# Exchanging the two operands of the output projection: weights stand, 512 gated values move

## The chip, the cores and the metric

The kernel runs on one core of a Trainium2 chip. The metric is the device time of one execution in microseconds (us). TensorE (PE) multiplies, its weight loads are listed apart (PEld), VectorE (DVE), ScalarE (ACT) and GpSimd (POOL) do the rest, and SyncE (SP) issues most of the transfers.

## The reference

Three layers follow each other. Only the third, a gated layer, is touched:

```python
def _moe2_ref(x, w_gate, w_val, w_out):
    g = x @ w_gate                       # 256 -> 1536
    silu = g * (1.0 / (1.0 + np.exp(-g)))
    val = x @ w_val
    return (silu * val @ w_out)          # 1536 -> 256

# x: 8 * 3072 tokens of 256 values. Ahead of it stand a spectral filter
# (rfft, times a filter, irfft) and a soft mixture of 8 experts with 4 slots
# each: x = softmax(logits, axis=1) @ slot_out, slot_out of 32 rows.
```

## The kernel before

Phase 1 (about the first 400 us) does the filter and the mixture's logits. On the side it rounds the three weight matrices of the gated layer (`conv`, lines 559 to 597): 36 chunks, 12 of them of `w_out` (index `i == 2`), go through ACT, DVE and POOL and are stored again in DRAM (`wd`, line 595), from where `first` (line 919) fetches `w_out` for phase 2. A short transition computes the slots' outputs times `w_gate` and `w_val`.

Phase 2 is a loop over 576 items `(b, q, G, f)`: 8 batches, 3 times 2 blocks of 512 tokens, and for each block 12 slices `f` of 128 hidden values. 12 items are a group, and a group makes 512 rows of the output. For an item,

- `gv` multiplies the slice of the gate and of the value matrix with the block's weights (two matmuls of 512 columns, lines 986 and 987), and ACT applies the silu (line 989);
- `gate` (DVE, line 995) multiplies both to `h`, and `split` one item later makes of it a rounded part `hi` (ACT, line 1002) and the rest `lo` (DVE, line 1003);
- `proj`, three or four items later (`lag`), multiplies with `w_out`. `wo[f]` holds two parts of it, index 0 the rounded one and index 1 the rest, made by `load_out` (lines 975 and 976) during the first 12 items.

`proj` computes `hi` times both parts of the weights and `lo` times the rounded part. `hi` and `lo` are the stationary operands, 128 tokens at a time (`t` from 0 to 3), and the weights move: 512 columns (both parts side by side) for `hi`, 256 for `lo`. Four PSUM banks `o0` to `o3` collect one group. At the end of a group ACT copies half of a bank (line 1027), DVE adds the other half to it (line 1028), and SP stores the 512 rows in four transfers (line 1031), each of 32 runs of 4 KB.

All engines take their instructions in the order in which the program is written (`manual_schedule`), so `proj(i - 4)` stands between `gv(i)` and `gate(i)`, and what it gives DVE at a group's end stands ahead of `gate(i)` there. The V tile in PSUM has two buffers (line 970): the matmul of line 987 for item `i + 2` waits until `gate(i)` has read the first.

Of the kernel before, what the change touches and what calls it, by code (L numbers as in the profile page):

```python
# [7 lines left out]
F32 = mybir.dt.float32  # L8
# [3 lines left out]
AF = mybir.ActivationFunctionType  # L12
ALU = mybir.AluOpType
# [4 lines left out]
NB, SEQ, D, E = 8, 3072, 256, 32  # L18
NEXP, SPE, FE, FF = 8, 4, 1024, 1536
NJ, NP, NR = 24, 96, 32  # L20
NF = FF // 128
# [58 lines left out]
def spectral_softmoe_glu_kernel(  # L80
# [17 lines left out]
    nc = tc.nc  # L98
    pe, dve, act, pool = nc.tensor, nc.vector, nc.scalar, nc.gpsimd
# [37 lines left out]
    def phase1():  # L137
        with ExitStack() as c1:
# [418 lines left out]
            def flat(a):  # L557
                return a.rearrange("(p a) f -> p (a f)", p=128)

            def conv():  # L560


                cw = 256
                chunks = [(i, c) for i in range(3) for c in range(FF * D // 128 // cw)]
                raws = {}

                def load(n):
                    if n >= len(chunks):
                        return
                    i, c = chunks[n]  # L570
                    raws[n] = cvp.tile([128, cw, 2], I32, tag="raw", name="raw", bufs=2)
                    nc.sync.dma_start(
                        out=raws[n].rearrange("p n k -> p (n k)"),
                        in_=flat((w_gate, w_val, w_out)[i])[:, c * cw:(c + 1) * cw].bitcast(I32),
                    )

                load(0)
                load(1)
                yield
                for n, (i, c) in enumerate(chunks):  # L580
                    raw = raws.pop(n)
                    hf, lw = raw[:, :, 1].bitcast(F32), raw[:, :, 0].bitcast(U32)
                    mag = cvp.tile([128, cw], I32, tag="mag", name="mag", bufs=2)
                    low = cvp.tile([128, cw], I32, tag="low", name="low", bufs=2)
                    act.activation(mag.bitcast(F32), hf, AF.Copy, scale=2.0 ** -112)
                    yield
                    act.activation(low, lw, AF.Copy, scale=2.0 ** -29)
                    act.activation(hf, hf, AF.Sign)
                    yield
                    dve.tensor_scalar(mag, mag, 3, None, ALU.logical_shift_left)  # L590
                    yield
                    pool.tensor_tensor(out=low, in0=mag, in1=low, op=ALU.add)
                    mf = low.bitcast(F32)
                    pool.tensor_tensor(out=mf, in0=mf, in1=hf, op=ALU.mult)
                    nc.sync.dma_start(out=flat(wd[i])[:, c * cw:(c + 1) * cw], in_=mf)
                    load(n + 2)
                    yield
# [55 lines left out]
            for k in range(2):  # L653
# [4 lines left out]
                out=nyq, in_=bass.AP(filt_r.tensor, SEQ // 2 * D, [[1, 128], [128, 2]])  # L658
# [7 lines left out]
            pool.tensor_scalar_mul(nyq, nyq, 0.5)  # L666
            dve.memset(expo, 0.0)
            side, firsts = conv(), first_weights()
            todo = []
            gens, ready = [], []  # L670
# [296 lines left out]
    def phase2(later):  # L967
        cp, g4, v4, wo, c4, build = (later[k] for k in ("cp", "g4", "v4", "wo", "c4", "build"))
        kp = p2.enter_context(tc.tile_pool(name="kp", bufs=3))
        ps_g = p2.enter_context(tc.tile_pool(name="ps_g", bufs=2, space=PSUM))  # L970
        ps_o = p2.enter_context(tc.tile_pool(name="ps_o", bufs=1, space=PSUM))

        def load_out(f):
            st = wo[f][:, 1, :].bitcast(F32)
            act.copy(wo[f][:, 0, :], st)
            pool.tensor_tensor(out=wo[f][:, 1, :], in0=st, in1=wo[f][:, 0, :], op=ALU.subtract)  # L976

        items = [(b, q, G, f) for b in range(NB) for q in range(3) for G in range(2) for f in range(NF)]
        hb, hhi, hlo, acc, sb2 = {}, {}, {}, {}, {}

        def gv(i):
            b, q, G, f = items[i]
            c, fs = f // 4, slice(f % 4 * 128, f % 4 * 128 + 128)
            pg = ps_g.tile([128, 512], F32, tag="G", name="G")
            pv = ps_g.tile([128, 512], F32, tag="V", name="V")
            pe.matmul(out=pg, lhsT=g4[c][:, fs], rhs=c4[b][:, q, G, :])  # L986
            pe.matmul(out=pv, lhsT=v4[c][:, fs], rhs=c4[b][:, q, G, :])  # L987
            s = kp.tile([128, 512], F32, tag="s", name="s")
            act.activation(s, pg, AF.Silu)  # L989
            sb2[i] = (s, pv)  # L990

        def gate(i):
            s, pv = sb2.pop(i)
            h = kp.tile([128, 512], F32, tag="h", name="h")
            dve.tensor_tensor(out=h, in0=pv, in1=s, op=ALU.mult)  # L995
            hb[i] = h

        def split(i):
            h = hb.pop(i)
            hi = kp.tile([128, 512], F32R, tag="hi", name="hi", bufs=LAG + 1)  # L1000
            lo = kp.tile([128, 512], F32R, tag="lo", name="lo", bufs=LAG + 1)
            act.copy(hi, h)  # L1002
            dve.tensor_tensor(out=lo, in0=h, in1=hi, op=ALU.subtract)  # L1003
            hhi[i], hlo[i] = hi, lo

        def proj(i):
            b, q, G, f = items[i]
            hi, lo = hhi.pop(i), hlo.pop(i)
            if f == 0:
                acc[0] = [ps_o.tile([128, 512], F32, tag=f"o{t}", name=f"o{t}") for t in range(4)]  # L1010
            for t in range(4):
                a = acc[0][t]
                ts = slice(128 * t, 128 * t + 128)
                pe.matmul(  # L1014
                    out=a, lhsT=hi[:, ts], rhs=wo[f].rearrange("p k d -> p (k d)"),
                    start=(f == 0), stop=(f == NF - 1), skip_group_check=True,
                )
                pe.matmul(  # L1018
                    out=a[:, D:2 * D], lhsT=lo[:, ts], rhs=wo[f][:, 0, :],
                    start=False, stop=(f == NF - 1), skip_group_check=True,  # L1020
                )
            if f == NF - 1:
                ot = kp.tile([128, 4, D], F32, tag="ot", name="ot", bufs=2)
                for t in range(4):
                    a = acc[0][t]
                    tmp = kp.tile([128, D], F32, tag="tmp", name="tmp", bufs=4)
                    act.copy(tmp, a[:, D:2 * D])  # L1027
                    dve.tensor_tensor(out=ot[:, t, :], in0=a[:, 0:D], in1=tmp, op=ALU.add)  # L1028
                row = b * SEQ + 1024 * q + 16 * G
                for ii in range(4):  # L1030
                    nc.sync.dma_start(
                        out=bass.AP(out.tensor, (row + 4 * ii) * D, [[32 * D, 32], [1, 4 * D]]),
                        in_=ot[32 * ii:32 * ii + 32].rearrange("p t d -> p (t d)"),
                    )

        def lag(i):

            r = i % (6 * NF) - EXP_AT
            if r in (1, 2, 3, 4, 5, 6):
                return (4, 3, 3, 3, 4, 4)[r - 1] if i < len(items) - 6 * NF else LAG  # L1040
            return min(LAG, 3 + i // 10)

        todo = list(range(len(items)))
        gen = build(1)
        for i in range(len(items) + LAG):
            if i < len(items):
                b, q, G, f = items[i]
                if q == 0 and G == 0 and f == 0 and b:
                    for _ in gen:
                        pass  # L1050
                    gen = build(b + 1) if b + 1 < NB else iter(())
                gv(i)
            while todo and todo[0] <= i - lag(i):
                proj(todo.pop(0))
            if i < len(items):
                gate(i)
            if i < NF:
                load_out(i)
            if 0 <= i - 1 < len(items):
                split(i - 1)  # L1060
            if i % 4 == 1 and i > NF:
                next(gen, None)

    with tc.manual_schedule():
        phase1()
        phase2(transition())
        p2.close()
# [32 lines left out]
```

## Time and profile before

| | |
|---|---|
| median of 3 runs | 1491.43 us (1491.24 to 1492.1) |
| the profiled execution, its own time | 1492.65 us |
| its span from the first to the last instruction | 1490.9 us |
| TensorE busy | 1439.6 us (97%) |
| VectorE busy | 1151.7 us (77%) |
| ScalarE busy | 962.5 us (65%) |
| stores of the output | 192 of 128 KB each |

The span is what the profile's views divide; the execution's own time is 1.75 us longer than the span, and lies 1.2 us above the median. A busy engine is not an engine at its peak: matmuls overlap in the records, so the time that one of them takes is read from the distance between starts, not from its own duration.

### The profile page before, as it was taken

Reading aid. Unit: us, or ns where it says so; the run is one execution under the profiler, and the core shown is the slowest. Engines: PE = TensorE matmul, PEld = TensorE weight load, DVE = VectorE, ACT = ScalarE, POOL = GpSimd, SP = SyncE. Lnnn points to the kernel's source line nnn. Section 1 sums busy time; section 2 is a strip of 40 time slices with the busy share of each in tenths; the row PEclk is TensorE's granted clock in tenths of the full one; section 3 lists DMA queues with packets and bytes.
Section 4 is the critical chain, followed back from the end, with each engine's and each line's share of the span. In section 5 each row is a group of like instructions: output and inputs, shape, how many; then the busy total and the mean of one; then the engine's idle time right before and its main releaser. Section 6 shows DMA issues by size and latency. Waiting matters only on the chain.

```text
span 1490.9 us, 25171 instructions
## 1 busy us (share of the span) xinstructions
PE 1439.6 (97%) x9574; PEld 1152.7 (77%) x9574; DVE 1151.7 (77%) x1870; ACT 962.5 (65%) x1838; POOL 241.9 (16%) x315
## 2 busy tenths in 40 slices
PE   4899999998899999999999999999999999999998
PEld 2566566665488888888888888888888888888887
DVE  2787888776378878878887887888789778877775
ACT  2476666663267667666766766676677667666665
POOL 0466667652110000000000000000000000000000
PEclk9999999999999999999999999999999999999999
DMA  9969878969711121121031012112111211111011
GB/s 226 160 119 157 157 136 146 174 152 382 243 27 29 44 54 29 43 54 29 15 71 39 15 37 64 26 29 57 40 29 27 59 40 28 44 43 27 17 29 29
DMA packets 87848, 116.42 MB, mean 78 GB/s; under 512 B 8880, under 2 KB 65072, under 8 KB 87600
## 3 DMA queue, kind: packets, MB, share of 16 engines
q1 hardware_dynamic: 80480, 102.37, 31.6%
q10 hardware_dynamic: 6800, 11.54, 2.6%
q8 instruction: 75, 1.23, 0.4%
q0 software_dynamic: 448, 0.92, 0.2%
q14 instruction: 45, 0.37, 0.1%
HBM read 68.13 MB, written 34.60 MB: 69 GB/s over the span
## 4 chain that ended last, share of the span: by engine, by line
PE 90%; DVE 4%; DMA 2%; ACT 2%; issue 1%; POOL 1%; ACTq 0%; POOLq 0%; DVEq 0%
PE o L1014 36%; PE o L1018 18%; PE V L987 9%; PE G L986 9%; PE X L258 5%; PE s L230 3%; PE T L283 2%; PE L L291 1%; PE c L482 1%; DMA fraw<-in_filt_i_dram 1%; DVE sg L238 1%; DMA nyq<-in_filt_r_dram 1%; PE c L364 1%; DVE P L262 1%; PE h L810 1%
## 5 line engine op out<-in xcount | busy, mean ns | idle before, releaser
L1014 PE MATMUL o<-wo,hi 128*128 128x512 f32 x2304 | 833.4, 396 | 2.7 <-POOL wo L976 2.7
L1018 PE MATMUL o<-wo,lo 128*128 128x256 f32 x2304 | 645.5, 280 | 0.0
L989 ACT ACTIVATE s<-G 128x512 f32<-128x512 f32 x576 | 344.7, 598 | 323.1 <-PE G L986 319.9
L995 DVE TENSOR_TENSOR h<-V,s 128x512 f32<-128x512 f32 x576 | 395.6, 687 | 171.7 <-ACT s L989 171.0
L1014 PEld LDWEIGHTS o<-wo,hi 128*128 128x128 f32 x2304 | 433.1, 188 | 106.8 <-POOL wo L976 3.0
L1018 PEld LDWEIGHTS o<-wo,lo 128*128 128x128 f32 x2304 | 434.8, 189 | 25.3
L1003 DVE TENSOR_TENSOR lo<-h,hi 128x512 fp32r<-128x512 f32 x576 | 423.2, 735 | 1.1
L1002 ACT CAST hi<-h 128x512 fp32r<-128x512 f32 x576 | 354.6, 616 | 11.7 <-DVE h L995 8.3
L987 PE MATMUL V<-c,v 128*128 128x512 f32 x576 | 227.7, 395 | 1.1 <-DVE h L995 1.1
L986 PE MATMUL G<-c,g 128*128 128x512 f32 x576 | 228.3, 396 | 0.2 <-ACT s L989 0.2
L258 PEld LDWEIGHTS X<-fwd,b 128*128 128x128 f32 x768 | 93.8, 192 | 56.7 <-issue 40.8
L986 PEld LDWEIGHTS G<-c,g 128*128 128x128 f32 x576 | 108.3, 188 | 26.2 <-ACT s L989 0.9
L238 DVE STREAM_TRANSPOSE sg<-s 128x1024 f32<-128x1024 f32 x64 | 79.0, 1237 | 60.8 <-PE s L230 59.2
L258 PE MATMUL X<-fwd,b 128*128 128x128 f32 x768 | 110.2, 287 | 1.7 <-ACT b L247 0.9
L987 PEld LDWEIGHTS V<-c,v 128*128 128x128 f32 x576 | 108.7, 189 | 3.1 <-DVE h L995 2.4
L933 POOL TENSOR_TENSOR lg<-lg,mx 96x1024 f32<-96x1024 f32 x7 | 16.8, 2406 | 565.8 <-DVE mx L931 565.8
L1028 DVE TENSOR_TENSOR ot<-o,tmp 128x256 f32<-128x256 f32 x192 | 70.0, 423 | 39.8 <-ACT tmp L1027 39.8
L247 ACT COPY b<-sg 128x768 f32<-128x768 f32 x64 | 59.1, 928 | 55.7 <-DVE sg L238 55.4
L230 PE MATMUL s<-x,csm 48*64 48x512 f32 x512 | 74.0, 641 | 19.0 <-DMA x<-in_x_dram 17.0
L271 POOL TENSOR_TENSOR yt<-P 128x256 f32<-128x256 f32 x96 | 70.3, 732 | 118.6 <-DVE P L262 117.9
L262 DVE TENSOR_TENSOR P<-X,ft 128x512 f32<-128x512 f32 x96 | 64.7, 674 | 11.0 <-PE X L258 10.6
L1027 ACT COPY tmp<-o 128x256 f32<-128x256 f32 x192 | 67.9, 372 | 4.3 <-PE o L1018 4.3
(197 smaller groups left out, 974.5 us busy)
## 6 DMA issues: line engine op xcount, KB each, us to landing
out_dram<-ot SPq DMA_DIRECT2D x192, 128.0 KB, 2.2
x<-in_x_dram SPq DMA_DIRECT2D x60, 384.0 KB, 8.3
w<-in_moe_w_dram SPq DMA_DIRECT2D x8, 1024.0 KB, 10.0
w<-in_moe_w_dram ACTq DMA_DIRECT2D x13, 512.0 KB, 7.3
c<-ch SPq DMA_DIRECT2D x42, 128.0 KB, 2.4
c<-cl SPq DMA_DIRECT2D x42, 128.0 KB, 2.4
raw<-in_moe_w_gate_dram SPq DMA_DIRECT2D x12, 256.0 KB, 6.0
raw<-in_moe_w_val_dram SPq DMA_DIRECT2D x12, 256.0 KB, 5.7
```

The lines of the kernel that those rows point to most:

```text
L230: pe.matmul(out=ps[64 * k:64 * k + 64, 16 * r:16 * r + 16, :], lhsT=s1t_sb[64 * r:64 * r + 48, :], rhs=xt[step][64 * r:64 * r + 48, k, :, ...
L238: dve.transpose(out=sg.rearrange("p j d k -> p d j k"), in_=ps.rearrange("p n d -> p d n"))
L258: pe.matmul(out=ps[:, g].rearrange("p r m -> p (r m)"), lhsT=bb[:, j, :], rhs=fwd[:, j, :])
L262: dve.tensor_tensor(out=P, in0=ps, in1=f, op=ALU.mult)
L986: pe.matmul(out=pg, lhsT=g4[c][:, fs], rhs=c4[b][:, q, G, :])
L987: pe.matmul(out=pv, lhsT=v4[c][:, fs], rhs=c4[b][:, q, G, :])
L989: act.activation(s, pg, AF.Silu)
L995: dve.tensor_tensor(out=h, in0=pv, in1=s, op=ALU.mult)
L1002: act.copy(hi, h)
L1003: dve.tensor_tensor(out=lo, in0=h, in1=hi, op=ALU.subtract)
L1014: pe.matmul(out=a, lhsT=hi[:, ts], rhs=wo[f].rearrange("p k d -> p (k d)"), start=(f == 0), stop=(f == NF - 1), skip_group_check=True,)
L1018: pe.matmul(out=a[:, D:2 * D], lhsT=lo[:, ts], rhs=wo[f][:, 0, :], start=False, stop=(f == NF - 1), skip_group_check=True,)
```

## The change

`proj` exchanges the operands: a slice of the weights stands (128 output columns, `h` 0 or 1), and all 512 tokens of `hi` or `lo` move. An item then has six matmuls of 512 columns in place of four of 512 and four of 256, and two banks collect a group in place of four; groups take `o0`, `o1` and `o2`, `o3` in turn (`accs`). The result stands in PSUM with output columns on partitions, so DVE turns each bank by 32x32 blocks straight into the tile `ot`; the copy of ACT and the addition of DVE are gone. For the turned tile to have neighbouring output columns side by side, `conv` stores the columns of `w_out` even ones first, then odd ones. A store now has 512 runs of 256 bytes. The last group keeps the old form (`close`), with its banks in the order 2, 3, 0, 1 and its addition undoing the new order of columns.

```diff
@@ conv, for each chunk of the three matrices
+                    halves = (lambda a: a.rearrange("p (m h) -> p h m", h=2)) if i == 2 else (lambda a: a)
+                    pair = (lambda a: a.rearrange("p (h m) -> p h m", h=2)) if i == 2 else (lambda a: a)
...
-                    act.activation(mag.bitcast(F32), hf, AF.Copy, scale=2.0 ** -112)
+                    act.activation(pair(mag.bitcast(F32)), halves(hf), AF.Copy, scale=2.0 ** -112)
...
-                    act.activation(low, lw, AF.Copy, scale=2.0 ** -29)
+                    act.activation(pair(low), halves(lw), AF.Copy, scale=2.0 ** -29)
...
-                    pool.tensor_tensor(out=mf, in0=mf, in1=hf, op=ALU.mult)
+                    pool.tensor_tensor(out=pair(mf), in0=pair(mf), in1=halves(hf), op=ALU.mult)
@@ proj
+        def accs(i):
+            if items[i][3] == 0:
+                n = i // NF % 2 * 2
+                tags = range(4) if i >= len(items) - NF else (n, n + 1)
+                acc[0] = {t: ps_o.tile([128, 512], F32, tag=f"o{t}", name=f"o{t}") for t in tags}
+            return acc[0]
+
         def proj(i):
             b, q, G, f = items[i]
             hi, lo = hhi.pop(i), hlo.pop(i)
-            for t in range(4):
-                a = acc[0][t]
+            a = list(accs(i).values())
...
+            for h in range(2):
+                w = wo[f].rearrange("p k (h m) -> p k h m", h=2)
+                for n, (k, m) in enumerate(((1, hi), (0, hi), (0, lo))):
+                    pe.matmul(
+                        out=a[h], lhsT=w[:, k, h], rhs=m,
+                        start=(f == 0 and n == 0), stop=(f == NF - 1 and n == 2), skip_group_check=True,
+                    )
+                if f == NF - 1:
+                    dve.transpose(
+                        out=ot[:, :, :, :, h].rearrange("p i t r -> p t i r"),
+                        in_=a[h].rearrange("p (t i s) -> p t i s", t=4, i=4),
+                    )
+            if f == NF - 1:
+                for ii in range(4):
+                    nc.sync.dma_start(
+                        out=bass.AP(out.tensor, row * D + 64 * ii, [[32 * D, 32], [D, 16], [1, 64]]),
+                        in_=ot[32 * ii:32 * ii + 32].rearrange("p i t r h -> p (i t) (r h)"),
+                    )
+
+        def close(i):
...
+            for t in (2, 3, 0, 1):
                 ts = slice(128 * t, 128 * t + 128)
                 pe.matmul(
-                    out=a, lhsT=hi[:, ts], rhs=wo[f].rearrange("p k d -> p (k d)"),
+                    out=a[t], lhsT=hi[:, ts], rhs=wo[f].rearrange("p k d -> p (k d)"),
...
-                    act.copy(tmp, a[:, D:2 * D])
-                    dve.tensor_tensor(out=ot[:, t, :], in0=a[:, 0:D], in1=tmp, op=ALU.add)
+                    act.copy(tmp, a[t][:, D:2 * D])
+                    dve.tensor_tensor(
+                        out=ot[:, t].rearrange("p (m h) -> p h m", h=2),
+                        in0=a[t][:, 0:D].rearrange("p (h m) -> p h m", h=2),
+                        in1=tmp.rearrange("p (h m) -> p h m", h=2),
+                        op=ALU.add,
+                    )
@@ the loop over items
-                proj(todo.pop(0))
+                n = todo.pop(0)
+                (close if n >= len(items) - NF else proj)(n)
```

On TensorE, the last item of a group and the first of the next read as follows in the program before (the number behind `o` is that of the bank's tile, `wo` the weights' tile, and a row ends with the output's partitions and columns):

```order
L986 MATMUL G<-c_6262,g_0_4827 128x512
L987 MATMUL V<-c_6262,v_0_4830 128x512
L1014 MATMUL o_6414<-wo_4835,hi 128x512
L1018 MATMUL o_6414<-wo_4835,lo 128x256
L1014 MATMUL o_6415<-wo_4835,hi 128x512
L1018 MATMUL o_6415<-wo_4835,lo 128x256
L1014 MATMUL o_6416<-wo_4835,hi 128x512
L1018 MATMUL o_6416<-wo_4835,lo 128x256
L1014 MATMUL o_6417<-wo_4835,hi 128x512
L1018 MATMUL o_6417<-wo_4835,lo 128x256
L986 MATMUL G<-c_6262,g_1_4828 128x512
L987 MATMUL V<-c_6262,v_1_4831 128x512
```

The same place on TensorE in the changed program, up to the first matmuls of the next group:

```order
L988 MATMUL G<-c_6104,g_0_4827 128x512
L989 MATMUL V<-c_6104,v_0_4830 128x512
L1026 MATMUL o_6465<-hi,wo_4835 128x512 x2
L1026 MATMUL o_6465<-lo,wo_4835 128x512
L1026 MATMUL o_6466<-hi,wo_4835 128x512 x2
L1026 MATMUL o_6466<-lo,wo_4835 128x512
L988 MATMUL G<-c_6104,g_1_4828 128x512
L989 MATMUL V<-c_6104,v_1_4831 128x512
L1026 MATMUL o_6694<-hi,wo_4833 128x512 x2
L1026 MATMUL o_6694<-lo,wo_4833 128x512
L1026 MATMUL o_6695<-hi,wo_4833 128x512 x2
L1026 MATMUL o_6695<-lo,wo_4833 128x512
```

Eight matmuls of 768 columns a pair became six of 512, the order of `gv` and `proj` stayed, and every matmul of the stretch now has 512 columns.

On VectorE, the end of a group before, with the four additions between `split` of one item and `gate` of the next:

```order
L995 TENSOR_TENSOR h<-V,s 128x512
L1003 TENSOR_TENSOR lo<-h,hi 128x512
L1028 TENSOR_TENSOR ot<-o_9349,tmp 128x256
L1028 TENSOR_TENSOR ot<-o_9350,tmp 128x256
L1028 TENSOR_TENSOR ot<-o_9351,tmp 128x256
L1028 TENSOR_TENSOR ot<-o_9352,tmp 128x256
L995 TENSOR_TENSOR h<-V,s 128x512
L1003 TENSOR_TENSOR lo<-h,hi 128x512
```

The end of a group on VectorE in the changed program:

```order
L997 TENSOR_TENSOR h<-V,s 128x512
L1005 TENSOR_TENSOR lo<-h,hi 128x512
L1031 STREAM_TRANSPOSE ot<-o_9002 128x4x4x32
L1031 STREAM_TRANSPOSE ot<-o_9003 128x4x4x32
L997 TENSOR_TENSOR h<-V,s 128x512
L1005 TENSOR_TENSOR lo<-h,hi 128x512
```

Two transposes of a whole bank stand where four additions of a half bank stood, ahead of the same `gate`.

## Rows read from the trace of the kernel before

**Rows 1.** The page: busy us (share of span), then TensorE busy and granted clock by slice.
```profile
PE 1439.6 (97%) x9574; PEld 1152.7 (77%) x9574; DVE 1151.7 (77%) x1870; ACT 962.5 (65%) x1838; POOL 241.9 (16%) x315
...
PE   4899999998899999999999999999999999999998
...
PEclk9999999999999999999999999999999999999999
```

**Rows 2.** Waits of TensorE from 430 us on: us, times, longest.
```profile
PE V L987 <- DVE h L995: 0.8, 2, 0.6
PE G L986 <- ACT s L989: 0.2, 1, 0.2
```

**Rows 3.** The chain that ended last from 930 to 1480 us, shares by line.
```profile
by line: PE o L1014 49.8%; PE o L1018 25.3%; PE V L987 12.5%; PE G L986 12.5%
```

**Rows 4.** Groups of TensorE from 930 to 1480 us: count, busy us, mean ns.
```profile
L1014 PE MATMUL o<-wo,hi 128*128 128x512 f32 x1181 | 426.1, 395 | 0.0
L1018 PE MATMUL o<-wo,lo 128*128 128x256 f32 x1181 | 330.4, 280 | 0.0
L986 PE MATMUL G<-c,g 128*128 128x512 f32 x295 | 116.6, 395 | 0.0
L987 PE MATMUL V<-c,v 128*128 128x512 f32 x295 | 116.2, 394 | 0.0
```

**Rows 5.** Timeline of SP: start us, us; stores of three groups, one after the other.
```profile
906.51 1.72 SPq L1031 DMA_DIRECT2D out_dram<-ot  x4
...
951.26 1.72 SPq L1031 DMA_DIRECT2D out_dram<-ot  x4
```

**Rows 6.** Timeline of TensorE where two items' `gv` follow each other: start us, us.
```profile
582.43 0.39 PE L986 MATMUL G<-c,g 128*128 128x512 f32 x1
582.66 0.40 PE L987 MATMUL V<-c,v 128*128 128x512 f32 x1
582.89 0.40 PE L986 MATMUL G<-c,g 128*128 128x512 f32 x1
583.13 0.39 PE L987 MATMUL V<-c,v 128*128 128x512 f32 x1
583.35 0.39 PE L1014 MATMUL o<-wo,hi 128*128 128x512 f32 x1
```

**Rows 7.** The chain at the very end, without `gv`: start us, us; ten pairs.
```profile
1480.92 0.24 PE o L1014
...
1484.10 0.24 PE o L1014
```

**Rows 8.** Groups of VectorE and ScalarE over the span: count, busy us, mean ns.
```profile
L1028 DVE TENSOR_TENSOR ot<-o,tmp 128x256 f32<-128x256 f32 x192 | 70.0, 423 | 39.8 <-ACT tmp L1027 39.8
...
L1027 ACT COPY tmp<-o 128x256 f32<-128x256 f32 x192 | 67.9, 372 | 4.3 <-PE o L1018 4.3
```

**Rows 9.** Groups of VectorE up to 430 us, by form: transposes of 512 columns.
```profile
L349 DVE STREAM_TRANSPOSE t<-c 128x512 f32<-128x512 f32 x16 | 10.4, 687 | 0.5 <-ACT lts L301 0.5
...
L633 DVE STREAM_TRANSPOSE ctf<-lgf 96x512 f32<-96x512 f32 x2 | 2.0, 1024 | 0.0
```

**Rows 10.** Timeline around a group's end, all engines: start us, us.
```profile
927.02 0.28 PE L1018 MATMUL o<-wo,lo 128*128 128x256 f32 x1
...
927.71 0.28 PE L1018 MATMUL o<-wo,lo 128*128 128x256 f32 x1
...
928.77 0.68 DVE L995 TENSOR_TENSOR h<-V,s 128x512 f32<-128x512 f32 x1
...
929.92 0.39 PE L987 MATMUL V<-c,v 128*128 128x512 f32 x1
```

**Rows 11.** The page: SP's DMA queue, packets, MB, share of 16 engines' span.
```profile
q1 hardware_dynamic: 80480, 102.37, 31.6%
```

**Rows 12.** Groups of GpSimd over the span: the two rounding steps, plain and with stride.
```profile
L594 POOL TENSOR_TENSOR low<-low,raw 128x256 f32<-128x256 f32 x36 | 27.0, 750 | 2.8
L592 POOL TENSOR_TENSOR low<-mag,low 128x256 int32<-128x256 int32 x36 | 26.3, 730 | 0.0
```

**Rows 13.** The rounding's last stores (first and last start) and the later load, from SP.
```profile
L595 SPq DMA_DIRECT2D wod<-low x12: 326/343/605, 247.7 to 318.4; - x12
...
387.04 2.31 SPq L919 DMA_DIRECT2D wo<-wod  x3
```

More of the change, by code (lines that the diff above doesn't have):

```diff
@@ L1008, in proj @@
             hi, lo = hhi.pop(i), hlo.pop(i)
-            if f == 0:
-                acc[0] = [ps_o.tile([128, 512], F32, tag=f"o{t}", name=f"o{t}") for t in range(4)]
-            for t in range(4):
-                a = acc[0][t]
+            row = b * SEQ + 1024 * q + 16 * G
+            a = list(accs(i).values())
+            ot = None
+            if f == NF - 1:
+                ot = kp.tile([128, 4, 4, 32, 2], F32, tag="ot", name="ot", bufs=2)
+            for h in range(2):
[10 more added lines that the diff above has]
+                    )
+            if f == NF - 1:
+                for ii in range(4):
[4 more added lines that the diff above has]
+        def close(i):
+            b, q, G, f = items[i]
+            hi, lo = hhi.pop(i), hlo.pop(i)
+            a = accs(i)
+            for t in (2, 3, 0, 1):
                 ts = slice(128 * t, 128 * t + 128)
                 pe.matmul(
-                    out=a, lhsT=hi[:, ts], rhs=wo[f].rearrange("p k d -> p (k d)"),
+                    out=a[t], lhsT=hi[:, ts], rhs=wo[f].rearrange("p k d -> p (k d)"),
                     start=(f == 0), stop=(f == NF - 1), skip_group_check=True,
@@ L1018, in proj @@
                 pe.matmul(
-                    out=a[:, D:2 * D], lhsT=lo[:, ts], rhs=wo[f][:, 0, :],
+                    out=a[t][:, D:2 * D], lhsT=lo[:, ts], rhs=wo[f][:, 0, :],
                     start=False, stop=(f == NF - 1), skip_group_check=True,
@@ L1023, in proj @@
                 ot = kp.tile([128, 4, D], F32, tag="ot", name="ot", bufs=2)
-                for t in range(4):
-                    a = acc[0][t]
+                for t in (2, 3, 0, 1):
                     tmp = kp.tile([128, D], F32, tag="tmp", name="tmp", bufs=4)
-                    act.copy(tmp, a[:, D:2 * D])
-                    dve.tensor_tensor(out=ot[:, t, :], in0=a[:, 0:D], in1=tmp, op=ALU.add)
+                    act.copy(tmp, a[t][:, D:2 * D])
[5 more added lines that the diff above has]
+                    )
                 row = b * SEQ + 1024 * q + 16 * G
```

## The prediction

> **What bounds the kernel now.** I read the page first: TensorE is busy 97% of the span, no other engine over 77%, and the granted clock is full nearly throughout [rows 1]. A busy matmul record may still hide a wait, so the second view is TensorE's own waits. From 430 us to the end they add up to 1.0 us in three waits [rows 2]. The third is the chain of waits from 930 to 1480 us: it never leaves TensorE, and its shares by line add up to the whole [rows 3]. So phase 2, some 1055 us of the span, is a stream of matmuls in which nothing waits. The reader is to see that work taken from ScalarE or VectorE is worth nothing here; only what a matmul takes of TensorE's stream counts.
>
> That price can be read three ways. Stores of output groups two apart start 44.75 us apart [rows 5]; 24 items lie between, so an item takes 1864.6 ns. The chain's shares of 550 us over the counts of its groups [rows 3, 4] give 273.9 us / 1181 = 231.9 ns for a 512-column matmul of `proj`, 139.15 / 1181 = 117.8 ns for one of 256, and 68.75 / 295 = 233.1 ns for G and V each. Over all 1771 of 512 columns that is 232.3 ns. Summed over an item (4 x 349.7 + 2 x 233.1) it is 1864.9 ns, which agrees with the stores. Half of 232.3 is 116.2, so a matmul pays at most some 3 ns for being an instruction of its own: time goes nearly by columns. Full clock is the 2.4 GHz level, at which 512 columns, one a clock, would be 213 ns; the stream is slower than that by 9%, and no wait or clock in the rows says why.
>
> **The change on TensorE.** Columns of an item stay: 4 x 768 = 3072 before, 6 x 512 = 3072 after, and 1024 for G and V. Two matmuls and two weight loads fewer are issued. An item becomes 8 matmuls of 512, so it costs 8 p, where p is the distance between starts in a stream of 512-column matmuls alone. 564 of the 576 items change (the last group keeps the old form), so the gain is 564 x (1864.6 - 8p) ns. The rows have no such stream; they bound p:
> - the mean of all 512-column matmuls in the mixed stream, 232.3 ns: 8p = 1858.4, a gain of 3.5 us;
> - the longest stretch without a 256 between, four starts in 0.92 us, 230 ns [rows 6]: 8p = 1840, a gain of 13.9 us. Starts are rounded to 0.01 us, so one stretch alone says 227.5 to 232.5;
> - the last items, where `gv` is over and only pairs of 512 and 256 run: nine pairs in 3.18 us, 353.3 ns a pair against 349.7 in the mixed stream, 1.0% slower [rows 7]. The pace thus depends on the sequence and not on columns alone. The same 1.0% on 232.3 is p = 234.7: 8p = 1877.6, a loss of 7.3 us.
>
> The sequences line up: the more 256s, the slower (353.3 against 349.7 a pair; 230 where four 512s follow each other). The new stream has none, so I leave the last bound as a rival and take the middle of the first two, p = 231.2 and 8p = 1849.6: 15.0 x 564 = 8.5 us gained.
>
> The Trainium skill ("TensorE: Matmul & The Clock Gate", section "Back-to-back issue gap") has a rule for this: at the full clock one matmul costs its columns over 2.4 plus 2.5 ns. By it 512 columns are an estimated 215.8 ns and 256 are 109.2, an item 1731.6 before and 1726.4 after, and the gain 564 x 5.2 = 2.9 us. The trace disagrees on the level (232.3 and 117.8).
>
> **Evictions.** Four copies of ScalarE (372 ns) and four additions of VectorE (423 ns) a group go [rows 8]; two transposes of 512 columns from PSUM come. No row has their output stride of two elements. The nearest are 687 ns (from PSUM) and 1024 ns (source in SBUF, strided) [rows 9]; I take 687, the one that also reads PSUM. VectorE then does 1.37 us in place of 1.69 a group. What stands behind them is `gate`, and V's next matmul waits for it. Around the group's end shown, the last `proj` matmul runs from 927.71 to 927.99, `gate` started at 928.77, and the V matmul that needs its buffer started at 929.92 [rows 10]. After: the second transpose runs 927.99 to 928.68, and `gate` ends 0.68 later at 929.36, 0.56 us ahead of need. The cover is gone when both transposes take over 0.97 us: the first bank is ready 0.70 us earlier, at 927.29, and 927.29 + 2 x 0.97 + 0.68 = 929.91. So the term is 0. Banks have a whole group of 22.4 us to be emptied, where before the first was written again within the next item; since TensorE did not wait for that either, this gains nothing. At most the 1.0 us of waits goes.
>
> **Stores.** A group's four stores become 2048 runs of 256 bytes, 128 for each of 16 engines. SP's queue took 31.6% of 16 x 1490.9 us for 80480 packets, 94 ns a packet of 1272 bytes on average [rows 11]. At that price, surely an upper bound if only size counts, a group's runs take 12 us of the 22.4 us until the next, and `ot` has two buffers. Behind them on SP's queue stand only the next batch's transfers of `build`, whose last has by the code 19 items (35 us) until its first use. Term 0.
>
> **Rounding and end.** Twelve chunks of `w_out` are read with a stride of four words instead of two. On GpSimd the step that has a stride today takes 750 ns, the plain one 730 [rows 12]; bounds are 0 and, doubled, 9 us over the whole stretch on an engine busy 16% of the span [rows 1]. The last of them was stored at 318.4 us and is loaded at 387 [rows 13], which covers it. The last group runs as before; if its final addition suffers from its stride, 0.4 us.
>
> Sum: 1492.65 - 8.5 = 1484.2 us for an execution like the profiled one, whose time is 1.2 us over the median; for the median **1483 us**.
>
> **Rivals.**
> 1. The 512s keep the pace that they have today, or slightly worse: p from 232.4 to 233.7. What is saved is at most two instructions of some 3 ns an item: 1488 to 1494 us. For it: the 232.3 ns rest on 1771 matmuls, the 230 on a few. The formula of the Trainium skill's page "TensorE: Matmul & The Clock Gate" ends here too, at an estimated 1488.5.
> 2. Slower: the stream falls into the slow repetition of the last items, p = 234.7, 1499 us. For it: those items are the only ones in the trace where `proj` stands alone, and no other engine was then at work that could slow it. Against: their pairs hold a 256. It decides from p = 233.7 on.
> 3. Slower: writing every second word makes a transpose as slow as the 1024 ns row. `gate` would end at 927.29 + 2.05 + 0.68 = 930.02, 0.1 us late, 47 times, +5 us: 1488 on top of the forecast's gain, 1496 without one; at twice 687 ns it is 0.8 us and +38 us.
> 4. Slower: a 256-byte run costs over 175 ns (22.4 us / 128), and stores hold up `ot`, the transposes and `gate`. At twice 94 ns a group would take 24.1 us: 47 x 1.7 = +80 us, 1563. Against: that is nearly twice the mean price of packets five times as long. The Trainium skill ("DMA: Bandwidth & Descriptors", "Specifications") does speak against such runs: transfers below 512 bytes are done by reading, changing and writing back. No run here shows such a store.
>
> **How the numbers follow.** 0.2% is 3 us, about what a measurement of this kernel can tell from no change. Faster by more than that needs p below 232.4, where the middle of my two bounds lies 1.2 ns inside: 0.62. Rival 1 is no change, 0.20. Rivals 2, 3 and 4 have 0.10, 0.03 and 0.05: slower 0.18. The range runs from p = 228.8 (a gain of 19.3 us, 1472, just above the low reading of the 512 stretch) to p = 234.0, 1496; rival 2's far part and rivals 3 and 4 stay out above it.
>
> **What the next profile would show.** An item is the distance of two groups' stores over 12: 1850 ns if the step on p is right, 1858 or more if rival 1 holds, 1870 and more for rival 2. TensorE should have no wait on `gate`'s or the silu's tiles worth 2 us in phase 2; if V's matmul waits on line 997 at each group's end, rival 3 holds, and if the transposes wait for transfers, rival 4. The transposes should take about 690 ns. I am wrong above all if p depends on something that the mixed stream does not show, such as which operand stands.

## The result and the profile after

The changed kernel takes 1466.01 us in the median of five runs (1462.54 to 1468.64), the kernel before 1491.43 beside it: a ratio of 0.983 (95% interval 0.981 to 0.984), 25.4 us less. The prediction said 1483 us, 1472 to 1496. The direction was right; the gain was three times the one forecast, and the time lies 6 us below the range.

The page of the changed kernel answers to [rows 1, 11]. Its first line gives busy us (share of the span) and instructions, its second packets, MB and the share of 16 engines' span. The profiled run's span is 1464.2 us, its own time 1466.01.

```profile
PE 1414.5 (97%) x8446; PEld 1101.4 (75%) x8446; DVE 1147.1 (78%) x1776; ACT 905.0 (62%) x1650; POOL 243.4 (17%) x315
...
q1 hardware_dynamic: 170720, 102.37, 35.6%
```

TensorE is still what bounds the kernel, with 1128 matmuls and as many weight loads fewer. SP's queue moves the same bytes in about twice the packets.

The waits of TensorE from 430 us to the end (us in total, times, longest us) answer to [rows 2]:

```profile
PE V L989 <- DVE h L997: 0.9, 2, 0.7
PE G L988 <- ACT s L991: 0.3, 1, 0.3
```

The chain of waits from 930 to 1440 us answers to [rows 3]; below it is one of its pieces (start us, us, what):

```profile
by line: PE o L1026 74.8%; PE V L989 12.5%; PE G L988 12.5%; PE o L1048 0.2%; PE o L1052 0.1%
...
965.56 2.72 PE o L1026 x12
```

Still hardly a wait in phase 2 (1.2 us in three), and every step of this chain is a matmul. G, V and each of the six matmuls of `proj` have the same share: 12.5% is one eighth, 74.8% six of them. Twelve matmuls in 2.72 us are 227 ns each. SP's stores (start us, us) give the item, as [rows 5] did:

```profile
895.17 2.19 SPq L1037 DMA_DIRECT2D out_dram<-ot  x4
...
938.69 2.18 SPq L1037 DMA_DIRECT2D out_dram<-ot  x4
```

43.52 us for 24 items are 1813.3 ns an item, 226.7 ns a matmul, where it was 1864.6. Times 564 items that is 28.9 us. The profiled run's span fell by 26.7 us only, since phase 2 began 2.1 us later (its first G matmul starts at 404.82 us against 402.67). That loss is in the last part of phase 1, as the windows from 330 to 372 us show: first the kernel before, then the changed one (us, busy us of each engine, granted clock, DMA share, GB/s).

```profile
330.00:372.00 42.00, 36.47 (x448) 23.85 (x447) 27.97 (x54) 17.54 (x35) 13.38 (x20) 1.00 0.91 341
```
```profile
330.00:372.00 42.00, 36.46 (x410) 23.55 (x412) 27.46 (x54) 17.52 (x35) 13.39 (x20) 0.92 0.86 327
```

On the timeline of TensorE (start us, us) one burst of 24 matmuls shows it, before and then after:

```profile
364.07 1.50 PE L482 MATMUL cl<-y,dh 128*32 128x256 f32 x24
...
369.03 0.35 PE L536 MATMUL psb<-al,csm 32*128 32x8 f32 x2 [0.42 <-DVE al L532]
```
```profile
364.68 2.79 PE L482 MATMUL cl<-y,dh 128*32 128x256 f32 x24
...
371.22 0.35 PE L536 MATMUL psb<-al,csm 32*128 32x8 f32 x2 [0.42 <-DVE al L532]
```

The same burst takes nearly twice as long: TensorE ran at its lower level, 1.2 GHz, for a part of this stretch. Ahead of it TensorE had the same short waits in both kernels (0.54, 0.34 and 0.62 or 0.63 us, from 358 to 361 us). Two runs of the next section tell whether the change is the cause. In e2_lo512, whose phase 1 is that of the kernel before, the burst is slow; in e6_runs4k, whose phase 1 is that of the changed kernel, it is fast:

```profile
365.65 2.79 PE L482 MATMUL cl<-y,dh 128*32 128x256 f32 x24
```
```profile
363.48 1.50 PE L482 MATMUL cl<-y,dh 128*32 128x256 f32 x24
```

The granted clock from 330 to 372 us is 0.92 in the first and 1.00 in the second, and phase 2 begins at 405.67 and 402.07 us. So the loss does not hang on the change: it is scatter of the clock from one execution to the next. Over the five runs of the changed kernel the spans spread from 1460.7 to 1466.8 us, with a mean granted clock from 0.995 down to 0.991.

### The profile page after: what moved, and what is told of

Same layout as the page of the kernel before. It is cut to its first block, busy times and chain, and to the rows that moved or that the text cites. A ratio compares the mean times of both kernels' runs of the same rounds, so it can differ in the third digit from the quotient of the medians.

```text
span 1464.2 us, 22633 instructions
## 1 busy us (share of the span) xinstructions
PE 1414.5 (97%) x8446; PEld 1101.4 (75%) x8446; DVE 1147.1 (78%) x1776; ACT 905.0 (62%) x1650; POOL 243.4 (17%) x315
## 3 DMA queue, kind: packets, MB, share of 16 engines
q1 hardware_dynamic: 170720, 102.37, 35.6%
## 4 chain that ended last, share of the span: by engine, by line
PE 91%; DVE 4%; ACT 2%; DMA 1%; issue 1%; POOL 1%; SPq 0%; ACTq 0%; POOLq 0%; DVEq 0%
PE o L1026 52%; PE V L989 9%; PE G L988 9%; PE X L258 5%; PE s L230 4%; PE T L283 2%; PE L L291 1%; PE c L482 1%; DMA x<-in_x_dram 1%; DVE sg L238 1%; PE o L1048 1%; PE c L364 1%; DVE P L262 1%; PE h L812 1%; PE c L447 1%
## 5 line engine op out<-in xcount | busy, mean ns | idle before, releaser
L1026 PE MATMUL o<-hi,wo 128*128 128x512 f32 x2256 | 696.3, 390 | 2.7 <-POOL wo L978 2.7
L1026 PEld LDWEIGHTS o<-hi,wo 128*128 128x128 f32 x2256 | 424.5, 188 | 91.3 <-POOL wo L978 3.0
L1026 PE MATMUL o<-lo,wo 128*128 128x512 f32 x1128 | 439.5, 390 | 0.0
L1026 PEld LDWEIGHTS o<-lo,wo 128*128 128x128 f32 x1128 | 212.0, 188 | 43.9
L988 PE MATMUL G<-c,g 128*128 128x512 f32 x576 | 224.7, 390 | 0.3 <-ACT s L991 0.3
L1031 DVE STREAM_TRANSPOSE ot<-o 128x512 f32<-128x512 f32 x94 | 65.1, 714 | 29.6 <-PE o L1026 29.6
L273 POOL TENSOR_TENSOR yt<-Q 128x256 f32<-128x256 f32 x95 | 69.5, 731 | 0.2
```

The costliest lines, as they stand in the source:

```text
L1026: pe.matmul(out=a[h], lhsT=w[:, k, h], rhs=m, start=(f == 0 and n == 0), stop=(f == NF - 1 and n == 2), skip_group_check=True,)
```

## Experiments

The theory formed after the result, called M in the expectations: a stream of matmuls of unequal lengths loses time against an even one, and moreover each matmul has a fixed price that the mixed stream hides. Its rivals: it matters which operand stands (O); each instruction, a matmul with its weight load, costs a fixed 26 ns, and the two that are gone are the whole gain (I); the old order of `hi` and `lo` had some other cost; or part of the gain lies outside TensorE. The table gives, from the starts in each trace, the sequence of columns in an item, the distance from one matmul to the next, and the item; the time of the kernel, and of the one before on the same chip.

| kernel | columns of an item after G and V | distances, ns | item, ns | us | before, us |
|---|---|---|---|---|---|
| before | 4 x (512, 256) | 224 to 241; 112 to 124 | 1864.6 | 1491.43 | |
| changed | 6 x 512 | 226 or 227 | 1813.3 | 1466.01 | 1491.43 |
| e1_sorted | 4 x 512, 4 x 256 | 226 to 237; 113 to 121 | 1860 inside a group | 1521.65 | 1492.96 |
| e2_lo512 | 8 x 512 | 225 to 228 | 2266.7 | 1725.32 | 1492.96 |
| e4_half | all 256 (16 an item) | 120 | 1920 | 1523.51 | 1492.96 |
| e5_mixed | 2 x (512, 512, 256, 256) | 226 to 236; 112 to 119 | 1847 | 1483.57 | 1492.96 |
| e7_pairs_old | 2 x (512, 512, 256, 256) | 226 to 239; 112 to 124 | 1847 inside a group | 1484.81 | 1492.37 |
| e8_alternate_new | 4 x (512, 256) | 224 to 241; 112 to 124 | 1864.4 | 1491.88 | 1492.37 |
| e9_stride | 6 x 512 | 230 (G, V), 233 | 1860 | 1489.86 | 1492.37 |
| e12_allstride | 6 x 512 | 233 or 234 | 1866.7 | 1492.97 | 1493.16 |
| e10_narrow | 6 x 512 | 224 to 236 | 1840 | 1476.63 | 1493.37 |

e1_sorted and e5_mixed ran four times, e9_stride and e3_close (below) twelve times, the others once. Runs of the same kernel lie up to 9 us apart (23 of the kernel before: 1488.35 to 1497.29 us), so where a kernel ran once, the item of its trace is the reading to go by.

**Uniform streams.** e2_lo512 leaves the kernel before as it is, but lets `lo` multiply both parts of the weights, so that all ten matmuls of an item have 512 columns and the gated values still stand:

```diff
-                    out=a[:, D:2 * D], lhsT=lo[:, ts], rhs=wo[f][:, 0, :],
+                    out=a, lhsT=lo[:, ts], rhs=wo[f].rearrange("p k d -> p (k d)"),
```

> The kernel before, with lo times both parts of the weights: its 256-column matmuls get 512 columns (a product that was left out is added), the gated values still stand. All ten matmuls of an item have 512 columns. M: 10 x 226.7 = 2267 ns an item, +232 us, 1723 us. O: the pace of the kernel before, 10 x 232.3 = 2323 ns, +264 us, 1755 us. I: 1024 more columns at 0.417 ns and no instruction more, 2291 ns, +246 us, 1737 us. Read from the distance of starts, M gives one constant 226.7, O a mean of 232.

TensorE's timeline (start us, us):

```profile
929.92 0.39 PE L1018 MATMUL o<-wo,lo 128*128 128x512 f32 x1
930.15 0.39 PE L1014 MATMUL o<-wo,hi 128*128 128x512 f32 x1
930.38 0.39 PE L1018 MATMUL o<-wo,lo 128*128 128x512 f32 x1
...
932.64 0.39 PE L1018 MATMUL o<-wo,lo 128*128 128x512 f32 x1
```

From 929.92 to 932.64 us lie twelve distances, 227 ns each, the changed kernel's own. Which operand stands makes no difference, and I, which asked for 2291 ns an item, fails. e4_half splits every matmul of the changed kernel's items in two of 256 columns:

```diff
-                    pe.matmul(
-                        out=a[h], lhsT=w[:, k, h], rhs=m,
...
+                    for c in (slice(0, 256), slice(256, 512)):
+                        pe.matmul(
+                            out=a[h][:, c], lhsT=w[:, k, h], rhs=m[:, c],
...
```

> The changed kernel with every matmul of the items in two halves of 256 columns (G and V too), weights standing; the last group keeps its old form in proj. One length only, 16 matmuls an item. M: one constant distance; 113.3 ns if the 226.7 of a 512 is all columns (1813 ns an item, 1466 us), 120 ns if its 13.3 ns above 512 clocks are paid by every matmul (1920 ns, 1526 us). O: 113.3 ns, 1466 us. I: eight instructions more at 26 ns, 2018 ns an item, 1581 us.

```profile
929.83 0.28 PE L1028 MATMUL o<-hi,wo 128*128 128x256 f32 x1
929.95 0.40 PE L1028 MATMUL o<-lo,wo 128*128 128x256 f32 x2
930.19 0.64 PE L1028 MATMUL o<-hi,wo 128*128 128x256 f32 x4
930.67 0.40 PE L1028 MATMUL o<-lo,wo 128*128 128x256 f32 x2
```

Seven matmuls start from 929.83 to 930.67 us: 120 ns each, constant over the whole of phase 2. With 226.7 for 512 this makes 106.7 ns for 256 columns, which is 2.4 columns a ns, the higher level of the clock, and 13.3 ns for each matmul at either length. I, which asked for 2018 ns an item, fails here too. At this fixed price an item of 4 x 226.7 + 4 x 120 + 2 x 226.7 would be 1840 ns in the kernel before; it was 1864.6.

**Order of lengths.** Three kernels keep the columns of before and change their order, with either operand standing. e5_mixed is the changed kernel with `lo` in two halves of 256, e7_pairs_old the kernel before with two banks' `hi` ahead of their `lo`, e8_alternate_new the changed kernel with the halves of `lo` between the others:

```diff
@@ e5_mixed, on the changed kernel
+                    for c in (slice(0, 512),) if n < 2 else (slice(0, 256), slice(256, 512)):
@@ e7_pairs_old, on the kernel before
-            for t in range(4):
+            for p in range(2):
+                for t in (2 * p, 2 * p + 1):
...
+                for t in (2 * p, 2 * p + 1):
@@ e8_alternate_new, on the changed kernel
-                for n, (k, m) in enumerate(((1, hi), (0, hi), (0, lo))):
+                for n, (k, m, c) in enumerate(((1, hi, whole), (0, lo, lower), (0, hi, whole), (0, lo, upper))):
```

> The changed kernel with only the lo matmul in two halves of 256: weights stand, but an item again has six matmuls of 512 and four of 256, in the order 512, 512, 256, 256. M: mixed lengths slow the stream again, 1840 to 1865 ns an item, 1481 to 1495 us, and the distances scatter. O: columns and operands are those of the changed kernel, 1813 ns, 1466 us. I: two instructions more, 1865 ns, 1495 us.

> The kernel before (gated values stand) with an item's matmuls in the order hi, hi, lo, lo, hi, hi, lo, lo, lengths 512, 512, 256, 256 as in e5_mixed. M, sharpened by the first four runs (in a stream of one length a matmul takes its columns at 2.4 GHz plus 13.3 ns; where lengths change, several matmuls lose more, as the order of the lengths alone decides): the 1847 ns an item of e5_mixed, 1481 us. O (the operand that stands has a part in what a change of length costs): nearer to the 1860 of e1_sorted and the 1865 of the kernel before, 1489 to 1492 us.

> The changed kernel (weights stand) with the lo matmul in two halves of 256, each behind a 512: the order 512, 256, 512, 256 of the kernel before. M: the 1865 ns an item of the kernel before, 1491 us. O: the 1847 ns of e5_mixed or less, 1481 us.

TensorE's timeline of e8_alternate_new, the weights standing:

```profile
931.41 0.28 PE L1027 MATMUL o<-lo,wo 128*128 128x256 f32 x1
931.54 0.39 PE L1027 MATMUL o<-hi,wo 128*128 128x512 f32 x1
931.77 0.28 PE L1027 MATMUL o<-lo,wo 128*128 128x256 f32 x1
931.88 0.39 PE L1027 MATMUL o<-hi,wo 128*128 128x512 f32 x1
932.12 0.28 PE L1027 MATMUL o<-lo,wo 128*128 128x256 f32 x1
```

The distances, 110 to 130 and 230 to 240 ns from these rounded starts, scatter as before. e8_alternate_new has the exchanged operands, the transposes, the new stores, and none of the gain: 1491.88 us beside 1492.37 of the kernel before, with the same pattern of distances. e5_mixed and e7_pairs_old, in pairs, both have 1847 ns an item inside a group, with opposite operands; e5_mixed measured 0.993 (0.992 to 0.995). The items at a group's end are longer in e7_pairs_old, so that its mean is 1851 ns. The G matmuls of two items that follow each other, in e5_mixed and then in e7_pairs_old (start us, us):

```profile
930.70 0.40 PE L988 MATMUL G<-c,g 128*128 128x512 f32 x1
...
932.55 0.40 PE L988 MATMUL G<-c,g 128*128 128x512 f32 x1
```
```profile
931.11 0.40 PE L986 MATMUL G<-c,g 128*128 128x512 f32 x1
...
932.96 0.40 PE L986 MATMUL G<-c,g 128*128 128x512 f32 x1
```

So the lengths and their order alone set the item: 1864.6 alternating, 1847 in pairs, 1840 by the fixed price alone.

e1_sorted goes further and puts all `hi` ahead of all `lo`:

> The kernel before, with the four hi matmuls of an item first and then its four lo matmuls; same operands, instructions and columns, only their order. Theory M (what slows the stream is that lengths of 512 and 256 alternate; a stretch of one length runs at 226.7 ns for 512, as after the change): six 512s follow each other, then four 256s, so an item takes about 6 x 226.7 + 4 x 120 = 1840 ns and the kernel 1477 us. Theory O (which operand stands and which moves decides): nothing changes, 1864.6 ns an item and 1491 us. Theory I (each instruction, matmul and weight load together, costs a fixed (1864.6 - 1813.3) / 2 = 26 ns): nothing changes, 1491 us.

It got slower, 1.020 (1.018 to 1.022). Inside a group an item takes 1860 ns, so larger runs of a length did not bring it nearer to 1840: M's forecast here was wrong, and the mere number of changes of length is not the law. The rest is a wait that the edit made: all four banks finish together, and the first `hi` of the next group waits until ScalarE and VectorE have emptied them. The chain of waits from 930 to 1480 us shows both engines where [rows 3] had none:

```profile
by line: PE o L1012 50.5%; PE o L1017 23.2%; PE V L987 11.3%; PE G L986 11.1%; DVE ot L1027 1.9%; ACT tmp L1026 1.7%; issue 0.4%
```

The item at a group's end takes 2.53 us, 0.67 more than the others; 47 of them are 31 us.

**The stored order of columns.** e3_close has the new order in `conv`, but the old operands throughout:

```diff
-                tags = range(4) if i >= len(items) - NF else (n, n + 1)
+                tags = range(4)
...
-                (close if n >= len(items) - NF else proj)(n)
+                close(n)
```

> The changed kernel with its last group's form for all groups: the order of the columns and the strided addition alone, operands as before. Items 1865 ns. If the 2 us by which the changed kernel enters the second phase later come from the rounding's strides, this one is 2 us over the kernel before; if they come from a stretch at the lower granted clock that does not hang on the change, it scatters with the kernel before, within 0 to 3 us.

1492.63 us beside 1492.37, a ratio of 1.000 (0.999 to 1.001), and phase 2 begins at 401.06 us. The rounding's strides cost the kernel nothing that these runs can tell (0.1%), though they do cost time on their engines. Groups of ScalarE from 240 to 320 us in the changed kernel (count, busy us, mean ns):

```profile
L589 ACT ACTIVATE low<-raw 128x256 int32<-128x256 uint32 x12 | 8.2, 685 | 0.7 <-issue 0.7
L587 ACT ACTIVATE mag<-raw 128x256 f32<-128x256 f32 x12 | 8.2, 682 | 2.3 <-DMA raw<-in_moe_w_out_dram 2.3
```

Both steps took 440 and 444 ns before, so ScalarE pays 24 x 0.24 = 5.8 us more there, hidden behind TensorE. The prediction costed GpSimd alone.

e9_stride is the opposite: the exchange without the stored order. A slice of standing columns is then read with a stride of two:

```diff
@@ conv
-                    halves = (lambda a: a.rearrange("p (m h) -> p h m", h=2)) if i == 2 else (lambda a: a)
+                    halves = (lambda a: a)
...
@@ proj
-                w = wo[f].rearrange("p k (h m) -> p k h m", h=2)
+                w = wo[f].rearrange("p k (m h) -> p k h m", h=2)
```

> The changed kernel without its first part: the columns of w_out are stored as they are, and the standing 128 columns are read with a stride of two instead; the last group's addition is the old one. If a weight load with that stride still hides behind the 226.7 ns of a matmul, 1813 ns an item as after the change. ScalarE's two steps of the rounding fall back from 0.68 to 0.44 us, 12 times each, which the first phase hides: the same time as the changed kernel, 1462 to 1468 us, or up to 2 us less. If the load is slower than 226.7 ns, the items are longer by what it lacks: at 300 ns, 564 x 8 x 0.073 = 330 us.

It nearly loses the whole gain: 0.998 (0.997 to 0.999), at 1860 ns an item, and both branches of the forecast missed. The groups of weight loads from 930 to 1440 us (count, busy us, mean ns):

```profile
L1026 PEld LDWEIGHTS o<-hi,wo 128*128 128x128 f32 x1098 | 212.2, 193 | 43.8
...
L988 PEld LDWEIGHTS G<-c,g 128*128 128x128 f32 x274 | 51.4, 188 | 11.0
```

A strided load takes 193 ns against 188, shorter than the matmul that it lies beside, and yet the matmuls move from 226.7 to 230 to 233 ns apart. What a load costs can't be read from its recorded length: e4_half's loads have no stride, are recorded at 192 ns and start 120 ns apart:

```profile
L1028 PEld LDWEIGHTS o<-hi,wo 128*128 128x128 f32 x2124 | 293.1, 192 | 0.0
```

e12_allstride tells whether that is the strided load's own price or that of a load unlike its neighbours: it lets G and V read strided columns as well, and assigns the rows of `w_out` to match.

```diff
-            pe.matmul(out=pg, lhsT=g4[c][:, fs], rhs=c4[b][:, q, G, :])
+            pe.matmul(out=pg, lhsT=g4[c][:, 256 * A:256 * A + 256].rearrange("p (m h) -> p h m", h=2)[:, B], rhs=c4[b][:, q, G, :])
...
```

> As the run without the stored column order, but G's and V's standing columns are read with a stride of two as well (and the hidden rows of w_out assigned to match), so that all eight weight loads of an item are alike. Two readings of that run's 230 to 234 ns. B: a load that differs from its neighbours (193 beside 188 ns) breaks the even beat, as a shorter load did: with all eight alike the distance is constant again at about 227 to 229 ns, an item 1815 to 1830 ns, 1465 to 1473 us. S: a load with a stride of two has a price of its own, a few ns each: eight of them make an item 1866 to 1872 ns (1860 for six, 1813 for none, so 7.8 a load), 1493 to 1497 us. I hold S the likelier, 60 to 40, since the distances were steady in that run and not scattered.

```profile
L1027 PEld LDWEIGHTS o<-hi,wo 128*128 128x128 f32 x1094 | 211.2, 193 | 44.1
...
L989 PEld LDWEIGHTS G<-c,g 128*128 128x128 f32 x273 | 52.7, 193 | 11.0
```

```profile
931.18 0.39 PE L990 MATMUL V<-c,v 128*128 128x512 f32 x1
...
933.05 0.39 PE L990 MATMUL V<-c,v 128*128 128x512 f32 x1
```

The first fence has the weight loads, the second (start us, us) the V matmuls of two items that follow each other, 1.87 us apart. All loads are alike at 193 ns, and the distance is even again, but at 233.3 ns: 1866.7 an item, 1492.97 us. The stride has a price of its own, 6.7 ns a matmul, and with it on all eight the exchange is worth nothing.

**Unequal loads.** e10_narrow keeps all matmuls at 512 columns, but loads 64 standing columns in place of 128 for `hi` times the weights' rest; it leaves out that product for the other 64 columns.

```diff
-                for n, (k, m) in enumerate(((1, hi), (0, hi), (0, lo))):
+                for n, (k, m, p) in enumerate(((0, hi, 128), (1, hi, 64), (0, lo, 128))):
                     pe.matmul(
-                        out=a[h], lhsT=w[:, k, h], rhs=m,
+                        out=a[h][0:p], lhsT=w[:, k, h, 0:p], rhs=m,
```

> The changed kernel with 64 standing columns in place of 128 for the product of hi and the weights' rest, the second of the three of a half; left out is that product for the other 64 columns. Columns that move and their number stay. Theory L (the 13.3 ns that a matmul takes over 512 clocks are what of a weight load is not hidden; the load with a stride, which raised them to 20, speaks for it): the matmul ahead of which or behind which the short load runs gets shorter, by up to half of 13.3 ns, twice an item: down to 1800 ns, 7.5 us off, about 1457 us. Theory F (a fixed price of a matmul, whatever its load): 226.7 ns throughout, 1813 ns, 1464 us.

```profile
L1026 PEld LDWEIGHTS o<-lo,wo 128*128 128x128 f32 x554 | 103.9, 188 | 52.1
L1026 PEld LDWEIGHTS o<-hi,wo 128*64 128x64 f32 x554 | 74.3, 134 | 23.9
```

```profile
929.97 0.39 PE L988 MATMUL G<-c,g 128*128 128x512 f32 x1
...
931.82 0.40 PE L988 MATMUL G<-c,g 128*128 128x512 f32 x1
```

Both forecasts missed. The load is 54 ns shorter, and the stream got slower: 1840 ns an item in the mean (above, one from G to G), 1476.63 us, with distances from 224 to 236 ns. So a stream of equal lengths loses its even beat too when the number of standing columns differs, even with less work in it. The matmul behind the short load also fills only 64 rows of its bank; whether load or matmul breaks the beat, this run does not tell.

**Outside TensorE.** e6_runs4k stores the same bytes in runs of 4 KB; the values land elsewhere in the output:

```diff
-                        out=bass.AP(out.tensor, row * D + 64 * ii, [[32 * D, 32], [D, 16], [1, 64]]),
-                        in_=ot[32 * ii:32 * ii + 32].rearrange("p i t r h -> p (i t) (r h)"),
+                        out=bass.AP(out.tensor, (row + 4 * ii) * D, [[32 * D, 32], [1, 4 * D]]),
+                        in_=ot[32 * ii:32 * ii + 32].rearrange("p i t r h -> p (i t r h)"),
```

> The changed kernel with its stores in 32 runs of 4 KB in place of 512 runs of 256 bytes; the same values go to other places in the output. If the short runs cost nothing, as the prediction had it: items at 1813 ns, the time of the changed kernel, 1462 to 1468 us. If they cost, items at the groups' ends get shorter and the time falls below 1462 us.

```profile
q1 hardware_dynamic: 80480, 102.37, 32.1%
```

Half the packets, 1463.54 us (before 1493.37), and still 1813.3 ns an item: runs of 256 bytes cost nothing here. e11_twice turns each bank twice:

```diff
-                    dve.transpose(
...
+                    for _ in range(2):
+                        dve.transpose(
...
```

> The changed kernel with each bank turned twice, the same values written again: 1.43 us more on VectorE at each group's end, ahead of gate. By the cover that the prediction gives gate (0.56 us; 0.54 us in the changed kernel's trace, 895.72 against 896.26 us), V's matmul then comes 1.43 - 0.54 = 0.9 us late 47 times, 42 us: 1508 us, with 47 waits of TensorE on gate. If VectorE's slack takes it up elsewhere, there are no such waits, and 1465 us.

Waits of TensorE from 430 us on:

```profile
PE V L989 <- DVE h L997: 38.8, 48, 1.1
```

1517.42 us. The wait is where the prediction put it and comes once for each of the 47 groups; the item at a group's end takes 2880 ns instead of 1813, so 47 x 1.07 = 50 us, where 42 were expected. By the starts in the trace V comes 0.93 us late, as forecast; the rest is in the matmuls behind the wait, the first of which is followed after 337 ns instead of 227.

## Why the prediction was wrong

**The step that failed is the size of p.** The structure held: only TensorE's stream counts, eight matmuls of 512 an item, gain 564 x (1864.6 - 8p). I took 231.2 ns and gave 228.8 as the end of the range; it is 226.7. The term is 28.9 us, not 8.5.

Both bounds that I took the middle of came from the mixed stream, and its unevenness is in both. It also misled me on what an instruction costs, in the sentence that "a matmul pays at most some 3 ns for being an instruction of its own: time goes nearly by columns". I halved the mixed stream's mean for 512 columns and compared it with the mean for 256 in the same stream. But alternation shifts both: a 512 is 5.6 ns slower there than in an even stream, a 256 2.2 ns faster (232.3 against 226.7, 117.8 against 120.0). The ratio came out near two, and hid both the fixed 13.3 ns (e4_half) and the loss by alternation. Of the 51.3 ns an item, two matmuls fewer are 26.7; the other 24.6 are the unevenness (1864.6 against 1840). The open remark "slower by 9%, and no wait or clock in the rows says why" was the place to stop: 9% of a stream without a wait was a price in search of a reason. (The sum over an item there is 1865.0 ns, not 1864.9; nothing rests on it.)

The Trainium skill ("TensorE: Matmul & The Clock Gate", "Back-to-back issue gap") gives 2.5 ns beside the columns, and calls this the gap of an isolated matmul; the prediction took it for a stream. In the even streams of these runs, each matmul with its load, it is 13.3 ns.

**The short stretch was not an even stream either.** The four distances of G and V in a row [rows 6] gave 230 ns with a lower reading of 227.5. In the changed kernel the same place reads:

```profile
580.06 0.39 PE L988 MATMUL G<-c,g 128*128 128x512 f32 x1
580.29 0.39 PE L989 MATMUL V<-c,v 128*128 128x512 f32 x1
580.52 0.39 PE L988 MATMUL G<-c,g 128*128 128x512 f32 x1
580.74 0.39 PE L989 MATMUL V<-c,v 128*128 128x512 f32 x1
580.97 0.62 PE L1026 MATMUL o<-hi,wo 128*128 128x512 f32 x2
```

That is 0.91 us in place of 0.92. In the nanoseconds of the traces it is 906 in place of 923, in steps of 226 or 227 in place of 230, 233, 236 and 224: four 512s in a row still pay for the 256s around them. The tail's pairs [rows 7] said rightly that pace depends on sequence, and I read them only as an upper bound. What I made of the sequences, "the more 256s, the slower", is wrong: with the same four 256s an item takes 1864.6 or 1847 ns by their order, and 256s alone have their even 120 ns (e4_half). The prediction's last sentence feared that p depends on something that the mixed stream does not show. It does: on evenness, and not on which operand stands.

**Evictions: right.** The changed kernel's timeline around a group's end (start us, us), to be held against [rows 10]:

```profile
893.74 1.40 DVE L1031 STREAM_TRANSPOSE ot<-o 128x512 f32<-128x512 f32 x2 [0.80 <-PE o L1026]
...
895.06 0.66 DVE L997 TENSOR_TENSOR h<-V,s 128x512 f32<-128x512 f32 x1
...
896.26 0.39 PE L989 MATMUL V<-c,v 128*128 128x512 f32 x1
```

`gate` ends at 895.72, 0.54 us ahead of V; forecast was 0.56. A transpose is 714 ns in the mean:

```profile
L1031 DVE STREAM_TRANSPOSE ot<-o 128x512 f32<-128x512 f32 x94 | 65.1, 714 | 29.6 <-PE o L1026 29.6
```

Rival 3's 1024 ns did not come, and e11_twice shows what lies beyond the cover.

**Stores: right.** 102.37 MB in 170720 packets at 35.6% are 49 ns a packet, half the bound of 94 that I used. A store lands after 2.8 us instead of 2.2. Rival 4 fell; the Trainium skill ("DMA: Bandwidth & Descriptors", "Specifications") speaks against runs below 512 bytes, and in e6_runs4k nothing was won by avoiding them.

**Rounding and end: right in the sum** (e3_close), though it left out ScalarE. Rival 1 and rival 2 are excluded by 226.7. Not forecast: the 2.1 us by which phase 2 began later, with the lower clock in its rows, which come without the change too (e2_lo512).

**What stays open:** why an uneven stream is slower. That the lengths and their order set it is shown, and that one short load with its matmul in a stream of 512s does it too; the rule is not, and e1_sorted (1860) against e5_mixed (1847) excludes the simple count of changes.

## What to carry to other kernels

Where TensorE runs without waits, compare the distance of starts with columns over the granted clock: what is left over is a price that can be bought back, by fewer matmuls and by giving all of them one length and one width of load. Take such a price only from a stream of the sequence that the new kernel will have; in a mixed one the means of long and short matmuls shift against each other. And keep standing columns side by side in SBUF: storing the weights in the order of use, for free here, was what kept the gain of the exchange.

## What the runs showed of the hardware

- An even stream of matmuls with a weight load each: 226.7 ns at 512 columns, 120.0 at 256, steady within 2 ns. In periods of 2.4 GHz that is 544 and 288, columns plus 32.
- With standing columns read at a stride of two it is 233.3 ns at 512 (560 periods, columns plus 48). The recorded length of the loads does not tell it: 193 ns there, 188 in the stream of 226.7 ns, and 192 without a stride where 256 columns move.
- Uneven lengths cost 7 to 25 ns an item of 1840 ns, by their order; a load of 64 columns among loads of 128 (its matmul filling 64 rows of the bank) costs 27 ns on 1813, though it is 54 ns shorter.
- Stores of 256-byte runs from SBUF: 49 ns a packet in the mean of the queue, nothing on the kernel's time.
